# Four more transposed chunks go through the DMA queue: two of the last attention's output, two of the next x

## The chip, the cores and the metric

The kernel runs on one core of a Trainium2 chip. The metric is the device time of one execution in microseconds (us), the median over several runs. The profile is of one execution; its span goes from the first to the last instruction.

Five engines work side by side, each on its own list of instructions in a fixed order: TensorE (PE, with its weight loads PEld), VectorE (DVE), ScalarE (ACT), GpSimd (POOL) and SyncE (SP), which here only issues DMAs. An instruction that must wait for another engine or for a DMA holds up everything behind it on its own engine.

## What is computed

```python
def reference(A_x, A_wqkv, A_wo, B_x, B_w1, B_w2):
    xn = layernorm(A_x)                       # 2048 x 640
    q, k, v = split(xn @ A_wqkv)              # 32 heads of 20
    idx = pos[:, None] - 2 * arange(8)[None]  # window of 8, dilation 2, masked below 0
    attn = softmax(einsum("bhsd,bhswd->bhsw", q, k[idx]) * 20 ** -0.5)
    s = einsum("bhsw,bhswd->bhsd", attn, v[idx]) @ A_wo
    g = silu(silu(xn @ B_w1) @ B_w2)          # 640 -> 1536 -> 640
    return A_x + s * g
```

`B_x` isn't used. Everything is float32. The kernel gets that accuracy from three products of split numbers: each matrix is held as a high part and a low part (the rest after rounding), and hi x hi, lo x hi and hi x lo are summed in PSUM.

## The kernel before

**Groups.** The 2048 positions are worked in four groups g = 0 to 3 of 512 (4 tiles of 128 rows). For each group comes `qkv_phase` (q, k and v in four quarters of 8 heads, q = 0 to 3, and the attention of each quarter on VectorE), then `ffn_phase` (12 up products, 12 down products). The attention of a group takes longer than its qkv products and runs on beside the group's FFN. The product with `wo` for group g - 1 is therefore done inside the FFN of group g, right after its first up product (`wo_phase`); for the last group it comes at the very end (`wo_last`).

**Turning.** A product wants its left side with the 640 channels on the partitions. So the normalised x and the attention's output O, both 128 rows x 640 channels a tile, must be turned, in five chunks c = 0 to 4 of 128 channels by 512 rows. Each chunk ends as a high part (TH, or OH for O) and a low part (TL, OL) in one of two slots that take turns. There are two ways:

- `split_t` (L620 and after): four 128x128 transposes on TensorE into one of two PSUM banks `rot` (L626); ACT copies the high part out (L630); for x, ACT also copies the whole (L632); DVE subtracts (L633 or L636). The up products use the same two `rot` banks.
- `turn_x`: ACT copies the float32 chunk as two planes of 16-bit halves into a buffer (L656); SP issues one DMA transpose for each plane into another buffer (L660); ACT copies the halves back together into the x tile (L665); ACT makes the high part (L670) and DVE the low part (L671). The buffers are pieces of the gate tile G, five of 512 columns, and one extra tile TURN. G is free from the time when `wo_phase` has multiplied it and POOL has added x to it (L1018) until the gate's silu at the end of the FFN (L1183). `X_BY` names which piece serves as source buffer: chunk 1 uses piece 2, chunk 3 piece 0, chunk 4 piece 1; chunks 0 and 2 use TURN. The result of chunk c lands in piece c.

`X_DMA` says which chunks of the next group's x are turned by DMA: in g = 1 all five, in g = 2 chunks 2, 3 and 4. In g = 0 none. The others are turned on TensorE after down products 1, 3, 5, 7 and 9. The chunks of O are turned on TensorE: those of groups 0 to 2 during the next group's qkv products (`O_AT`), those of g = 3 in its own FFN, chunk 0 after down 5, chunk 1 after down 7, chunk 2 after down 8, and chunks 3 and 4 (`o_rest`, L818) before and in the last up product.

**Weights.** A ring of seven slots holds weight units. When a unit's products end, `w_load` starts the load of the unit seven later: from half copies kept in DRAM by POOL's queue (L562), or from the raw weights with a split on ACT and DVE or POOL.

**Attention on DVE.** Per quarter and pair of tiles: q times k (L719), sum over a head (L722), softmax in small steps, weights times v (L761), and a tree of sums into O (L767, L772, L774). For the pairs named in `SHARED`, the last two sums run on POOL, on the quarter's used-up keys: the plane `KV[q][:, 0]`, seen as `partial(q)`.

**The order.** Nothing of the order is written by hand except TensorE's. Each operation is added with its engine, an estimated duration, what it reads and writes, a priority, an earliest time (`at`) and, for DMAs, its bytes. `Weave.order` then simulates the five engines and lists the operations by simulated start; a locked operation keeps DVE and POOL apart. `Weave.plan` repeats this up to 90 times and adds constraints where TensorE would stand idle in the simulation. `clock[0]` is the sum of the TensorE work added so far. A DMA transpose is simulated as 2.0 us of SP and 8 us on top of the usual landing.

Of the kernel before, what the change touches and what calls it, by code (L numbers as in the profile page):

```python
# [10 lines left out]
U16 = mybir.dt.uint16  # L11
AF = mybir.ActivationFunctionType
# [3 lines left out]
P = 128  # L16
# [5 lines left out]
CQ = HQ * DH  # L22
J = 8
T = 4
TOK = T * P
# [27 lines left out]
OUT_IN = 6.0  # L53
CARRY_AT = 8.0
X_SINGLE = (1,2,)
X_DMA = {1: (0, 1, 2, 3, 4), 2: (2, 3, 4)}
X_BY = {1: 2, 3: 0, 4: 1}
SLOW, ISSUE, SUB_LATE = 8, 2.0, 3
PACE0, PACE = -20.0, 12.0
BACK = {1: 0.0, 2: 40.0}  # L60
QAT = 48
OAT = 16
STORE_Q = 1, 3
# [257 lines left out]
def local_attention_silu_ffn(ctx: ExitStack, tc: tile.TileContext, x, wqkv, wo, w1, w2, out):  # L321
    nc = tc.nc
# [18 lines left out]
    NG = len(groups)  # L341
# [15 lines left out]
    TH = [sb.tile([P, DC * TOK + OAT], F32R, name="th0")]  # L357
# [4 lines left out]
    TL = tiles("tl", 2, [P, DC * TOK + 64], F32R)  # L362
    chunks = lambda tiles, at: [v[:, at:at + DC * TOK].rearrange("p (c n) -> p c n", c=DC) for v in tiles]
    OH, OL = chunks(TH, OAT), chunks(TL, OAT)
    TH, TL = chunks(TH, 0), chunks(TL, 0)
# [6 lines left out]
    KV = tiles("kv", NQ, [P, 2, HALO + T, CQ])  # L372
    Q = tiles("q", NQ, [P, T, CQ])
    E = [v[:, :, CQ - W * HQ:].rearrange("p t (w h) -> p t w h", w=W) for v in Q]
    O = sb.tile([P, T, D], F32, name="o")
    PR = sb.tile([P, 2, W, CQ], F32, name="pr")
    L = tiles("l", 2, [P, T, W, HQ])
    XIN = sb.tile([P, T, D], F32, name="xin")
    G = sb.tile([P, T, D], F32, name="gate")
# [3 lines left out]
    TURN = sb.tile([P, TOK], F32, name="turn")  # L383
# [29 lines left out]
    def act(n, fn, reads, writes, prio, table=None, more=0.0, late=0.0, at=0.0, spans=()):  # L413
        return add("ACT", ac(n) + more, fn, reads, writes, prio, table=table, late=late, at=at, spans=spans)

    def free_for(old, new):

        add("DVE", 0.0, lambda: None, [], list(old) + list(new), 0)
# [8 lines left out]
    clock = [0.0]  # L427
# [214 lines left out]
    def both(k):  # L642
        return [k + (0,), k + (1,)]

    def chunk_span(of, c, write=False):
        return [(of, c * P, (T - 1) * D + (c + 1) * P, write)]

    def piece(tile_of, k):
        return tile_of.rearrange("p t d -> p (t d)")[:, k * TOK:(k + 1) * TOK]

    def turn_x(c, i, at, back):

        keys = [("xin", t) for t in range(T)]
        (a, ka), (b, kb) = (piece(G, X_BY[c]), ("buf", X_BY[c])) if c in X_BY else (TURN, ("turn",)), (piece(G, c), ("buf", c))
        into = XIN[:, :, c * P:(c + 1) * P]
        act(2 * TOK, lambda: nc.scalar.activation(  # L656
            a.bitcast(U16).rearrange("p (h t n) -> p h t n", h=2, t=T), into.bitcast(U16).rearrange("p t (n h) -> p h t n", h=2),
            AF.Copy), keys, both(ka), 150, at=at, spans=chunk_span("x", c))
        for h in range(2):
            dma(lambda h=h: nc.sync.dma_start_transpose(  # L660
                b.bitcast(U16).rearrange("p (h t n) -> p h t n", h=2, t=T)[:, h],
                a.bitcast(U16).rearrange("p (h n) -> p h n", h=2)[:, h]),
                [ka + (h,)], [kb + (h,)], P * TOK * 6, clock[0], ISSUE, SLOW)
        kh, kl = t_keys(i, [c], kinds=["th"]), t_keys(i, [c], kinds=["tl"])
        act(2 * TOK, lambda: nc.scalar.activation(  # L665
            into.bitcast(U16).rearrange("p t (n h) -> p h t n", h=2),
            b.bitcast(U16).rearrange("p (h t n) -> p h t n", h=2, t=T), AF.Copy),
            both(kb) + keys, [("xw", c)], 150, more=0.3, at=back, spans=chunk_span("x", c, True))
        hi, lo = (v[i][:, c, :].rearrange("p (t n) -> p t n", t=T) for v in (TH, TL))
        act(TOK, lambda: nc.scalar.activation(hi, into, AF.Copy), [("xw", c)] + keys, kh, 0)  # L670
        dve(TOK, lambda: nc.vector.tensor_tensor(out=lo, in0=into, in1=hi.bitcast(F32), op=OP.subtract),  # L671
            [("xw", c)] + keys + kh, kl, 0, lock=True, late=SUB_LATE, spans=chunk_span("x", c))

    def tile_spans(of, cs, ts):
        return [(of, t * D + c * P, t * D + (c + 1) * P, False) for t in ts for c in cs]
# [32 lines left out]
    def halo_keys(q):  # L708
        return [("halo", q, 1, 0), ("halo", q, 1, 112), ("halo", q, 2, 0), ("halo", q, 2, 112), ("halo", q, 3, 0),
                ("halo", q, 4, 0)] + [("kv", q, t) for t in range(T)]  # L710
# [93 lines left out]
    def o_chunk(g, c, i):  # L804
        qs = range(c * P // CQ, ((c + 1) * P - 1) // CQ + 1)
        split_t(O, [("o", q, t) for q in qs for t in (0, 2)], c, i, (OH, OL))
# [104 lines left out]
    def qkv_phase(g, i, io):  # L911
        for q in range(NQ):
            if g == 0 and q == 0:
                ps = first_quarter(i)
            else:
                ps = [bank() for t in range(T)]
                for c in range(DC):
                    wh, wl, kh, kl = w_next("q", q, c)
                    for t in range(T):
                        o, kp = ps[t]  # L920

                        def unit(c=c, t=t, o=trio_sums(o), wh=wh, wl=wl):
                            hi, lo = TH[i][:, c, tsl(t)], TL[i][:, c, tsl(t)]
                            vh, vl = trio(wh), trio(wl)
                            nc.tensor.matmul(o, hi, vh, start=c == 0, stop=False)  # L925
                            nc.tensor.matmul(o, lo, vh, start=False, stop=False)  # L926
                            nc.tensor.matmul(o, hi, vl, start=False, stop=c == DC - 1)  # L927
                        pe(3 * mm(3 * CQ), unit, t_keys(i, [c], [t]) + [kh, kl], [kp])
                    w_done()
                    if g:  # L930
                        for k in O_AT.get((q, c), ()):
                            o_chunk(g - 1, k, io)
            if groups[g][0] == 0:
                zero = KV[q][0:2, 0:2 - g, 0:HALO, :]
                add("POOL", 2.0 - g, lambda zero=zero: nc.gpsimd.memset(zero, 0.0), [] if g or not q else ["first"],
                    [("halo", q, 1, 0), ("halo", q, 2, 0), ("halo", q, 3, 0), ("halo", q, 4, 0)], clock[0] if g else 1 + 12 * q)
            for t in range(T):
                evac_qkv(g, q, t, *ps[t])
            halo(g, q)
            attend(g, q)  # L940
        attend(g, NQ)

    def t_keys(i, cs, ts=range(T), kinds=("th", "tl")):
        return [(k, i, c, t) for k in kinds for c in cs for t in ts]
# [37 lines left out]
    def gate(ts, cs):  # L982
        return of(G[:, ts.start] if ts.stop - ts.start == 1 else G[:, ts], cs)

    def gkeys(ts, cs):
        return [("g", t, cs.start) for t in range(ts.start, ts.stop)]
# [158 lines left out]
    def ffn_phase(g, i, ix, io):  # L1145
        if g + 1 < NG:
            behind = [("kv", XQ, 0)] if g else []
            step = 1 if g in X_SINGLE else 2
            for t in range(0, T, step):
                load_x(g + 1, t, step, behind=behind)  # L1150
            for t in range(T):
                ln_stats(t)
            ln_rstd(0, T)
            for t in range(T):
                ln_apply(t)
        ps = None
        by_dma = X_DMA.get(g, ())
        bufs = [("buf", c, h) for c in range(DC) for h in range(2)]
        for kind, f in plan(g):
            if kind == "w1":  # L1160
                up(g, i, f, io)
            elif kind == "wo":
                wo_phase(g - 1, io)
                if g == NG - 1:
                    free_for([("xin", t) for t in range(T)], [("xin", t, c) for t in range(T) for c in (0, CA)])
                for c in range(DC) if by_dma else ():
                    ts = slice(c * TOK // D, ((c + 1) * TOK - 1) // D + 1)
                    free_for(gkeys(ts, slice(0, CA)) + gkeys(ts, slice(CA, D)), bufs[2 * c:2 * c + 2])
                for k, c in enumerate(by_dma):
                    turn_x(c, ix, clock[0] + PACE0 + PACE * k, clock[0] + BACK[g])  # L1170
            elif kind == "x":
                if f not in by_dma:
                    split_t(XIN, [("xin", t) for t in range(T)], f, ix, (TH, TL), XIN[:, :, tsl(f)])
            elif kind == "o":
                o_chunk(g, f, io)
            elif kind == "rest":
                o_rest(g, f, io)
            else:
                ps = ps or tm_banks()
                down(f, ps)  # L1180
        for p, kp, ts, cs in tm_views(ps):
            n = (ts.stop - ts.start) * (cs.stop - cs.start)
            act(n, lambda p=p, ts=ts, cs=cs: nc.scalar.activation(gate(ts, cs), p, AF.Silu), [kp], gkeys(ts, cs) + bufs * bool(by_dma), 0, "silu")  # L1183

    add("POOL", 0.7, consts, [], ["consts"], 0)
    act(1, lambda: nc.scalar.activation(SD[:, 1, 0:1], epst, AF.Sqrt), ["consts"], [("rs", 0)], 0, "sqrt")
# [37 lines left out]
```

## Time and profile before

| | us |
|---|---|
| median of 3 runs | 602.38 (601.88 to 603.2) |
| the profiled execution | 600.52 |
| its span | 598.7 |
| DVE busy | 515.6 |
| ACT busy | 236.9 |
| POOL busy | 163.5 |
| transposes of O on TensorE (L626) | 72 |
| transposes of x on TensorE (L626) | 28 |
| DMA transposes (L660) | 16 |

The profile gives times from the start of the span. A row of a view of groups or of the time line names the line of the code, the engine, the operation, what it writes and reads, and in brackets the idle time before it with what ended that. "SPq" and "POOLq" are the queue's own instructions, such as the issue of a DMA. The granted clock of TensorE is 1.00 throughout. The three later FFN phases lie at about 189 to 284 (g = 1), 335 to 431 (g = 2) and 481 to 576 us (g = 3); the last `wo` product follows from 576.

### The profile page before, as it was taken

How to read it: one execution, taken by the hardware profiler on the slowest of the kernel's cores; microseconds unless marked ns; L12 is line 12 of the kernel's file. 1: busy time of each engine (PE TensorE's matmuls, PEld its weight loads, DVE VectorE, ACT ScalarE, POOL GpSimd, SP SyncE). 2: the span in 40 equal slices, each digit the busy share in tenths (PEclk: the TensorE clock that was granted, in tenths of full speed). 3: DMA queues.
4: the chain of work that ended last, by engine and by line, in shares of the span. 5: the costliest groups of instructions: out<-in, count | busy, mean ns of one | idle time of the engine just before them, and what ended most of it. 6: DMA issues, size and time to landing. Idle time of an engine off the chain costs nothing.

```text
span 598.7 us, 9085 instructions
## 1 busy us (share of the span) xinstructions
PE 593.2 (99%) x3463; PEld 558.4 (93%) x3463; DVE 515.6 (86%) x505; ACT 236.9 (40%) x434; POOL 163.5 (27%) x229
## 2 busy tenths in 40 slices
PE   8999999999999999999999999999999999999997
PEld 7999999999999999999999999999999999999997
DVE  6599999999799978999979999999828799999544
ACT  5447364453546224555324604452412342313230
POOL 5800102233110153433211137433122133441100
PEclk9999999999999999999999999999999999999999
DMA  9999999779999999965699999997689997766652
GB/s 295 305 315 335 323 409 387 299 244 299 275 330 313 324 256 334 250 211 164 184 336 293 308 360 269 274 265 223 211 219 284 295 332 247 242 193 215 198 181 88
DMA packets 74823, 162.90 MB, mean 272 GB/s; under 512 B 14509, under 2 KB 38797, under 8 KB 74781
## 3 DMA queue, kind: packets, MB, share of 16 engines
q1 hardware_dynamic: 54941, 82.62, 47.4%
q0 software_dynamic: 19296, 79.31, 44.5%
q8 instruction: 27, 0.44, 0.3%
q10 hardware_dynamic: 544, 0.41, 0.2%
q14 instruction: 15, 0.12, 0.1%
HBM read 107.91 MB, written 34.16 MB: 237 GB/s over the span
## 4 chain that ended last, share of the span: by engine, by line
PE 98%; DMA 1%; DVE 0%; issue 0%
PE acc L969 22%; PE acc L971 15%; PE acc L925 10%; PE acc L926 10%; PE acc L927 10%; PE rot L1104 9%; PE rot L1106 9%; PE rot L1105 9%; PE acc L875 2%; PE rot L626 2%; DMA xin<-in_A_x_dram 1%; PE rot L859 0%; PE rot L1087 0%; DVE st L844 0%; PE rot L818 0%; DVE gate L1055 0%
## 5 line engine op out<-in xcount | busy, mean ns | idle before, releaser
L925 PE MATMUL acc<-w,th 128*128 128x480 f32 x300 | 110.8, 369 | 0.0
L926 PE MATMUL acc<-w,tl 128*128 128x480 f32 x300 | 109.8, 366 | 0.0
L927 PE MATMUL acc<-w,th 128*128 128x480 f32 x300 | 109.8, 366 | 0.0
L969 PE MATMUL acc<-w,sh 128*128 128x384 f32 x384 | 108.6, 328 | 0.0
L719 DVE TENSOR_TENSOR pr<-q,kv 128x2560 f32<-128x2560 f32 x32 | 90.2, 2819 | 18.1 <-ACT th L630 13.0
L971 PE MATMUL acc<-w,sh 128*128 128x256 f32 x384 | 104.7, 273 | 0.0
L1104 PE MATMUL rot<-th,w 128*128 128x512 f32 x240 | 92.1, 384 | 0.0
L761 DVE TENSOR_TENSOR pr<-q,kv 128x2560 f32<-128x2560 f32 x32 | 90.7, 2834 | 1.1
L1105 PE MATMUL rot<-tl,w 128*128 128x512 f32 x240 | 91.0, 379 | 0.0
L1106 PE MATMUL rot<-th,w 128*128 128x512 f32 x240 | 91.0, 379 | 0.0
L722 DVE TENSOR_REDUCE l<-pr 128x128 f32<-128x2560 f32 x32 | 89.6, 2801 | 0.2
L1117 ACT ACTIVATE sh<-rot 128x512 fp32r<-128x512 f32 x48 | 28.8, 599 | 138.5 <-PE rot L1106 138.4
L562 POOL DMA_DIRECT2D w<-half_w x72 | 38.8, 539 | 156.5 <-PE acc L971 56.8
L971 PEld LDWEIGHTS acc<-w,sh 128*128 128x128 f32 x384 | 73.7, 192 | 0.6
L969 PEld LDWEIGHTS acc<-w,sh 128*128 128x128 f32 x384 | 72.6, 189 | 0.6
L562 POOL DMA_DIRECT2D w<-half_q x52 | 27.8, 535 | 122.9 <-PE acc L927 75.4
L927 PEld LDWEIGHTS acc<-w,th 128*128 128x128 f32 x300 | 56.7, 189 | 4.0
L926 PEld LDWEIGHTS acc<-w,tl 128*128 128x128 f32 x300 | 56.7, 189 | 3.8
L925 PEld LDWEIGHTS acc<-w,th 128*128 128x128 f32 x300 | 56.7, 189 | 3.8
L969 PE MATMUL acc<-w,sl 128*128 128x384 f32 x192 | 55.9, 328 | 0.0
L1119 DVE TENSOR_TENSOR sl<-sf,sh 128x512 fp32r<-128x512 f32 x48 | 42.0, 876 | 14.3 <-ACT sf L1118 14.1
L971 PE MATMUL acc<-w,sl 128*128 128x256 f32 x192 | 52.3, 273 | 0.0
(106 smaller groups left out, 1059.9 us busy)
## 6 DMA issues: line engine op xcount, KB each, us to landing
w<-half_w POOLq DMA_DIRECT2D x72, 640.0 KB, 5.5
w<-half_q POOLq DMA_DIRECT2D x52, 480.0 KB, 4.9
half_w<-w SPq DMA_DIRECT2D x24, 640.0 KB, 6.2
half_q<-w SPq DMA_DIRECT2D x20, 480.0 KB, 6.7
kv<-kv SPq DMA_DIRECT2D x15, 560.0 KB, 8.1
w<-half_wo POOLq DMA_DIRECT2D x10, 640.0 KB, 7.0
kv<-kv SPq DMA_DIRECT2D x15, 420.0 KB, 8.3
gate<-in_B_w_dram SPq DMA_DIRECT2D x16, 320.0 KB, 6.9
```

The costliest lines, as they stand in the source:

```text
L562: add("POOL", 1.0, lambda: nc.gpsimd.dma_start(both, src), [("half", u)], [kh, kl], due + 10, nbytes=2 * n * P * 4)
L719: dve(2560, lambda: nc.vector.tensor_tensor(out=PR, in0=win(qq[:, t:t + 2, :], W, 0), in1=win(kv[:, 0, t:t + 2, :], W, CQ), op=OP.mult), h ...
L722: dve(2560, lambda: nc.vector.tensor_reduce(out=l[:, t:t + 2].rearrange("p t w h -> p (t w h)"), in_=PR.rearrange("p t w (h d) -> p (t w h ...
L761: dve(2560, lambda: nc.vector.tensor_tensor(out=PR.rearrange("p t w (h d) -> p t (w h) d", d=DH), in0=e[:, t:t + 2].rearrange("p t w h -> ...
L925: nc.tensor.matmul(o, hi, vh, start=c == 0, stop=False)
L926: nc.tensor.matmul(o, lo, vh, start=False, stop=False)
L927: nc.tensor.matmul(o, hi, vl, start=False, stop=c == DC - 1)
L969: nc.tensor.matmul(a[t][0][:, :CA].rearrange("p (m h) -> p m h", h=2), st, col_a(w), start=first, stop=last)
L971: nc.tensor.matmul(b[t // 2][0][:, h * CB:(h + 1) * CB].rearrange("p (m h) -> p m h", h=2), st, col_b(w), start=first and h == 0, stop=las ...
L1104: nc.tensor.matmul(to, wh[:, cs], hi, start=c == 0, stop=False)
L1105: nc.tensor.matmul(to, wh[:, cs], lo, start=False, stop=False)
L1106: nc.tensor.matmul(to, wl[:, cs], hi, start=False, stop=c == DC - 1)
```

## The change

1. `X_DMA[2]` becomes all five chunks: in g = 2, x chunks 0 and 1 of the last group are no longer turned on TensorE after downs 1 and 3 but by DMA. `BACK[2]`, the earliest time of the copies back after the `wo` product, goes from 40 to 0 us.
2. `O_DMA` is new: in g = 3, chunks 0 and 1 of O are turned by DMA. Their buffers are two halves of the key plane `KV[c][:, 0]` of quarter c, lent out once its last reader is done (`lend`, `spare`). The copy out comes at the earliest 10 and 25 us after the FFN began, the copy back at 40 and 55. The result is written into OH and OL of the slot that `wo_last` reads.
3. `turn_x` is split into `send` (copy out, two DMA transposes) and `join` (copy back, high part, low part), which `turn_o` uses too. The priority of a DMA transpose on SP is now the time of its own copy plus 2, where it was the TensorE clock at the end of `wo_phase`; that holds for g = 1 as well. `O_OUT` and `O_BACK` of groups 1 and 2 are not used, as `O_DMA` names g = 3 alone.

```diff
-X_DMA = {1: (0, 1, 2, 3, 4), 2: (2, 3, 4)}
+X_DMA = {1: (0, 1, 2, 3, 4), 2: (0, 1, 2, 3, 4)}
+O_DMA = {3: (0, 1)}
+O_OUT = (), (35.0, 55.0), (35.0, 55.0), (10.0, 25.0)
+O_BACK = (), (80.0, 82.0), (80.0, 82.0), (40.0, 55.0)
-BACK = {1: 0.0, 2: 40.0}
+BACK = {1: 0.0, 2: 0.0}
...
+    def send(src, c, keys, of, by, to, at):
+        (a, ka), (b, kb) = by, to
         act(2 * TOK, lambda: nc.scalar.activation(
...
-                [ka + (h,)], [kb + (h,)], P * TOK * 6, clock[0], ISSUE, SLOW)
+                [ka + (h,)], [kb + (h,)], P * TOK * 6, at + 2, ISSUE, SLOW)
+    def join(to, into, kinto, reads, c, i, dest, at, spans=((), ())):
...
+    def turn_o(c, i, by, to, at, back):
+        qs = range(c * P // CQ, ((c + 1) * P - 1) // CQ + 1)
+        send(O, c, [("o", q, t) for q in qs for t in (0, 2)], "o", by, to, at)
+        join(to, by[0].rearrange("p (t n) -> p t n", t=T), both(by[1]), [], c, i, (OH, OL), back)
+
+    def turn_os(g, i, begun):
+        by_dma = O_DMA.get(g, ())
+        for c in by_dma:
+            lend(c)
+        for k, c in enumerate(by_dma):
+            turn_o(c, i, spare(c, 0), spare(c, 1), begun + O_OUT[g][k], begun + O_BACK[g][k])
+        for c in by_dma:
+            lend(c, True)
+
+    def spare(q, k):
+        return KV[q][:, 0].rearrange("p t m -> p (t m)")[:, k * TOK:(k + 1) * TOK], ("spare", q, k)
+
+    def lend(q, back=False):
+        old = [(k, q, t) for k in ("kv", "own", "val") for t in range(T)] + [("partial", q)] + halo_keys(q)
+        new = [k for p in range(2) for k in both(("spare", q, p))]
+        free_for(*((new, old) if back else (old, new)))
...
                 wo_phase(g - 1, io)
                 if g == NG - 1:
+                    turn_os(g, io, begun)
...
             elif kind == "o":
-                o_chunk(g, f, io)
+                if f not in O_DMA.get(g, ()):
+                    o_chunk(g, f, io)
```

More of the change, by code (lines that the diff above doesn't have):

```diff
@@ L649, in piece @@
         return tile_of.rearrange("p t d -> p (t d)")[:, k * TOK:(k + 1) * TOK]
[L651 to L655, printed above, removed]
+    def send(src, c, keys, of, by, to, at):
+        (a, ka), (b, kb) = by, to
         act(2 * TOK, lambda: nc.scalar.activation(
-            a.bitcast(U16).rearrange("p (h t n) -> p h t n", h=2, t=T), into.bitcast(U16).rearrange("p t (n h) -> p h t n", h=2),
-            AF.Copy), keys, both(ka), 150, at=at, spans=chunk_span("x", c))
+            a.bitcast(U16).rearrange("p (h t n) -> p h t n", h=2, t=T),
+            src[:, :, c * P:(c + 1) * P].bitcast(U16).rearrange("p t (n h) -> p h t n", h=2),
+            AF.Copy), keys, both(ka), 150, at=at, spans=chunk_span(of, c))
         for h in range(2):
@@ L662, in turn_x @@
                 a.bitcast(U16).rearrange("p (h n) -> p h n", h=2)[:, h]),
-                [ka + (h,)], [kb + (h,)], P * TOK * 6, clock[0], ISSUE, SLOW)
-        kh, kl = t_keys(i, [c], kinds=["th"]), t_keys(i, [c], kinds=["tl"])
+                [ka + (h,)], [kb + (h,)], P * TOK * 6, at + 2, ISSUE, SLOW)
+    def join(to, into, kinto, reads, c, i, dest, at, spans=((), ())):
+        b, kb = to
         act(2 * TOK, lambda: nc.scalar.activation(
@@ L667, in turn_x @@
             b.bitcast(U16).rearrange("p (h t n) -> p h t n", h=2, t=T), AF.Copy),
-            both(kb) + keys, [("xw", c)], 150, more=0.3, at=back, spans=chunk_span("x", c, True))
-        hi, lo = (v[i][:, c, :].rearrange("p (t n) -> p t n", t=T) for v in (TH, TL))
-        act(TOK, lambda: nc.scalar.activation(hi, into, AF.Copy), [("xw", c)] + keys, kh, 0)
+            both(kb) + reads, kinto, 150, more=0.3, at=at, spans=spans[0])
+        kh, kl = t_keys(i, [c], kinds=["th"]), t_keys(i, [c], kinds=["tl"])
+        hi, lo = (v[i][:, c, :].rearrange("p (t n) -> p t n", t=T) for v in dest)
+        act(TOK, lambda: nc.scalar.activation(hi, into, AF.Copy), kinto + reads, kh, 0)
         dve(TOK, lambda: nc.vector.tensor_tensor(out=lo, in0=into, in1=hi.bitcast(F32), op=OP.subtract),
-            [("xw", c)] + keys + kh, kl, 0, lock=True, late=SUB_LATE, spans=chunk_span("x", c))
+            kinto + reads + kh, kl, 0, lock=True, late=SUB_LATE, spans=spans[1])
+    def turn_x(c, i, by, to, at, back):
+        keys = [("xin", t) for t in range(T)]
+        send(XIN, c, keys, "x", by, to, at)
+        join(to, XIN[:, :, c * P:(c + 1) * P], [("xw", c)], keys, c, i, (TH, TL), back,
+             (chunk_span("x", c, True), chunk_span("x", c)))
+    def turn_o(c, i, by, to, at, back):
[16 more added lines that the diff above has]
+        free_for(*((new, old) if back else (old, new)))
     def tile_spans(of, cs, ts):
@@ L931, in qkv_phase @@
                         for k in O_AT.get((q, c), ()):
-                            o_chunk(g - 1, k, io)
+                            if k not in O_DMA.get(g - 1, ()):
+                                o_chunk(g - 1, k, io)
             if groups[g][0] == 0:
@@ L1156, in ffn_phase @@
         ps = None
+        begun = clock[0]
         by_dma = X_DMA.get(g, ())
@@ L1164, in ffn_phase @@
                 if g == NG - 1:
+                    turn_os(g, io, begun)
+                if g == NG - 1:
                     free_for([("xin", t) for t in range(T)], [("xin", t, c) for t in range(T) for c in (0, CA)])
@@ L1169, in ffn_phase @@
                 for k, c in enumerate(by_dma):
-                    turn_x(c, ix, clock[0] + PACE0 + PACE * k, clock[0] + BACK[g])
+                    by = (piece(G, X_BY[c]), ("buf", X_BY[c])) if c in X_BY else (TURN, ("turn",))
+                    turn_x(c, ix, by, (piece(G, c), ("buf", c)), clock[0] + PACE0 + PACE * k, clock[0] + BACK[g])
             elif kind == "x":
@@ L1183, in ffn_phase @@
             act(n, lambda p=p, ts=ts, cs=cs: nc.scalar.activation(gate(ts, cs), p, AF.Silu), [kp], gkeys(ts, cs) + bufs * bool(by_dma), 0, "silu")
+        if g < NG - 1:
+            turn_os(g, i, begun)
     add("POOL", 0.7, consts, [], ["consts"], 0)
```

## The prediction

> **What bounds the kernel now.** I read the page first, then the waits of PE, then the chain in order of time at the places that the change touches, then the three FFN stretches by windows. The group numbers below are those of the code, g = 0 to 3.
>
> ```profile
> PE 593.2 (99%) x3463; PEld 558.4 (93%) x3463; DVE 515.6 (86%) x505; ACT 236.9 (40%) x434; POOL 163.5 (27%) x229
> PE 98%; DMA 1%; DVE 0%; issue 0%
> ```
>
> TensorE is busy 593.2 of 598.7 us, and 98% of the chain that ended last is TensorE. The waits of PE name only these:
>
> ```profile
> PE rot L831 <- POOL ident masks.py:199: 1.4, 1, 1.4
> PE rot L859 <- DVE xin L849: 0.2, 1, 0.2
> ```
>
> Both lie in the first quarter (warm-up and first tiles). After that TensorE never waits. So the time is a plain sum of TensorE work, and work taken off TensorE comes out of the time in full, unless the replacement makes TensorE wait somewhere.
>
> **What is removed.** Four chunks leave TensorE: x chunks 0 and 1 in the FFN of g = 2, and o chunks 0 and 1 in the FFN of g = 3. Each is four 128x128 transposes. The chain in order of time (start, length) has exactly these four:
>
> ```profile
> 367.73 0.44 PE rot L626 x4
> 384.45 0.44 PE rot L626 x4
> 540.28 0.44 PE rot L626 x4
> 553.78 0.44 PE rot L626 x4
> ```
>
> The chain counts from the end of one piece to the end of the next, so 0.44 is what one chunk takes from TensorE, and 4 x 0.44 = **1.76 us** go. No more than that can be won, since TensorE waits for nothing that could get shorter.
>
> **What is added, on ACT and DVE.** The groups by form:
>
> ```profile
> L630 ACT ACTIVATE th<-rot 128x512 fp32r<-128x512 f32 x25 | 14.9, 596 | 57.8 <-PE rot L626 57.8
> L632 ACT ACTIVATE xin<-rot 128x512 f32<-128x512 f32 x7 | 4.1, 592 | 0.0
> L633 DVE TENSOR_TENSOR tl<-xin,th 128x512 fp32r<-128x512 f32 x7 | 4.8, 685 | 1.4 <-ACT xin L632 1.4
> L656 ACT ACTIVATE gate<-xin 128x1024 uint16<-128x1024 uint16 x5 | 5.2, 1050 | 2.7 <-POOL xr L1018 2.7
> L665 ACT ACTIVATE xin<-gate 128x1024 uint16<-128x1024 uint16 x8 | 10.9, 1366 | 0.0
> L670 ACT ACTIVATE th<-xin 128x512 fp32r<-128x512 f32 x8 | 5.1, 632 | 0.3
> L671 DVE TENSOR_TENSOR tl<-xin,th 128x512 fp32r<-128x512 f32 x8 | 6.0, 744 | 0.0
> ```
>
> A chunk turned by DMA costs ACT 1.05 + 1.37 + 0.63 = 3.05 us. An x chunk gives back 0.60 + 0.59, so g = 2 gains 2 x 1.86 = 3.7 us of ACT; an o chunk gives back 0.60, so g = 3 gains 2 x 2.45 = 4.9. DVE gains about 0.06 a chunk. The three FFN stretches (length, then busy time of PE, PEld, DVE, ACT and POOL, granted clock, DMA share, GB/s):
>
> ```profile
> 189.00:284.00 95.00, 95.00 (x592) 90.17 (x591) 85.20 (x70) 41.74 (x59) 34.25 (x48) 1.00 0.95 260
> 335.00:431.00 96.00, 96.00 (x599) 91.15 (x599) 91.01 (x71) 39.55 (x58) 35.05 (x49) 1.00 1.03 276
> 481.00:576.00 95.00, 95.00 (x596) 90.13 (x595) 84.72 (x73) 27.99 (x44) 28.75 (x43) 1.00 0.75 231
> ```
>
> ACT is busy 40 of 96 us in the second and 28 of 95 in the third, so it has room; the PE column is full in all three. The first stretch, g = 1, already turns all five chunks by DMA with the same steps, and PE waits for nothing there. That is the nearest row for g = 2, and I cost the ACT and DVE work at **0**. The cover is the lead of each up product over its down product. Gone it is where ACT sits in a wait with a silu (L1117) queued behind it: a rival below. The changed priorities on SP touch g = 1 too, with the same instructions: 0, and no further bound than the rivals'.
>
> **What is added, on SP and the DMA engines.** Eight transposes, two per chunk:
>
> ```profile
> L660 SPq DMA_TRANSPOSE gate<-turn x6: 1202/1438/1930, 215.2 to 367.6; - x6
> gate<-gate SPq DMA_TRANSPOSE x10, 8.5
> ```
>
> Each holds SP 1.2 to 1.9 us and lands about 8.5 us after issue. In g = 3 SP has nothing to issue between these two rows, and o of heads' quarter 1 is whole when POOL ends its last sum:
>
> ```profile
> 485.14 2.06 SPq L1011 DMA_DIRECT2D xr<-in_A_x_dram  x3
> 523.86 0.87 POOL L774 TENSOR_TENSOR o<-kv 128x320 f32<-128x320 f32 x1
> 563.00 0.33 SPq L1028 DMA_DIRECT2D pr<-in_A_x_dram  x1
> 575.86 0.49 ACT L1183 ACTIVATE gate<-acc 128x384 f32<-128x384 f32 x1 [2.91 <-PE acc L969]
> ```
>
> The later chunk (o 1) then runs 524.7 + 1.05 (copy) + 2.9 (two issues) + 8.5 + 1.37 + 0.63 + 0.74 = about 540. Its reader, the last wo product, comes after the gate's first silu at 575.9: 36 us of margin. The keys of quarters 0 and 1, which lend their planes, have their last reader at the same 524.7. Cost 0.
>
> In g = 2 the readers are the products of g = 3. In g = 1 the last subtraction of a turned chunk, and the first gate silu of that stretch, were
>
> ```profile
> 277.49 0.68 DVE L671 TENSOR_TENSOR tl<-xin,th 128x512 fp32r<-128x512 f32 x1
> 281.65 0.49 ACT L1183 ACTIVATE gate<-acc 128x384 f32<-128x384 f32 x1 [6.20 <-PE acc L969]
> 428.10 0.49 ACT L1183 ACTIVATE gate<-acc 128x384 f32<-128x384 f32 x1 [1.48 <-PE acc L969]
> 430.93 0.53 POOL L562 DMA_DIRECT2D w<-half_q  x1 [2.76 <-PE acc L971]
> 433.37 0.53 POOL L562 DMA_DIRECT2D w<-half_q  x1 [1.91 <-PE acc L927]
> ```
>
> Moved by 428.10 - 281.65 = 146.45, it ends at about 424.6. TensorE enters g = 3 at about 430.9 and takes 2.44 us a chunk (the two POOL rows, each let go by a finished unit), so chunk 4 is read at 440.7: 16 us of margin. Cost 0.
>
> **The one thin margin** is a weight load in g = 2. The ring has seven slots, so a load that starts when a unit ends is for the unit seven later. The load at 368.03 follows the second down product and is for down 5. The rows: the load; the landings of the loads issued between 365.5 and 368.5, and of all loads from 180 to 300 (g = 1); SP beside it; a window; and the end of a down unit, 3.29 before the one at 430.93:
>
> ```profile
> 368.03 0.53 POOL L562 DMA_DIRECT2D w<-half_w  x1 [1.83 <-PE rot L626]
> DMA to landing us min/median/max: 8.8/11.7/14.7
> DMA to landing us min/median/max: 3.5/5.1/8.9
> 366.13 2.96 SPq L660 DMA_TRANSPOSE gate<-turn  x2
> 372.00:376.00 4.00, 4.00 (x20) 3.52 (x19) 3.90 (x4) 1.08 (x2) 2.40 (x4) 1.00 1.32 73
> 427.64 0.53 POOL L562 DMA_DIRECT2D w<-half_q  x1 [2.76 <-PE acc L971]
> ```
>
> The second row holds two loads: the earlier one landed after 8.8, the later one, with two transposes issued beside it, after 14.7, at 382.7. From 372 to 376 the DMA engines moved 73 GB/s, against 276 in the whole stretch, and were busy all along. Down 5 comes after the turn of x 1 (384.45 + 0.44 = 384.89) and one down product (3.29): at 388.2. With both turns gone it comes at 387.3, which leaves 387.3 - 382.7 = **4.6 us**. Now chunk 0's two transposes stand where chunk 2's stood and chunk 1's two follow. What these two more cost the load has no row. Least: 0, since in g = 1, where the same five chunks are turned, no load took over 8.9. Most by the row: 14.7 - 8.8 = 5.9 again, a stall of 1.3. I take no stall, as g = 1 is the nearer row in what it turns; the end of 1.3 goes into the range.
>
> The Trainium skill, "Advanced Engine Details and Errata", section "X-Bar Transpose (TRN2)", holds transposing DMAs to be as fast as regular ones. By that rule the two added would take the load well under 2 us and the margin would stay. The 73 GB/s beside the transposes speak against it.
>
> Two waits are moved. POOL's add of row 3 waits for an x load that SP issues behind the first transposes, and a weight load stands behind the add; on SP the x loads for the last wo product (L1049) wait for the last subtraction:
>
> ```profile
> 369.89 0.35 SPq L1017 DMA_DIRECT2D xr<-in_A_x_dram  x1
> 383.40 1.55 POOL L1018 TENSOR_TENSOR xr<-xr,gate 128x640 f32<-128x640 f32 x1 [1.41 <-DMA xr<-in_A_x_dram]
> 387.51 0.57 POOL L562 DMA_DIRECT2D w<-half_w  x1
> SPq L1049 <- DVE tl L671: 23.7, 2, 17.6
> ```
>
> Two more issues put the x load 2.9 us back and the weight load to 390.4. It is for the unit seven after the one that ended at 384.45, due six units of 3.29 later, at 404.2; with a landing of 8.8 it is there at 399: cost 0 (with one of 14.7, 0.9 us, which the range holds). Behind L1049 stand the carry loads and key shifts of g = 3; those need quarter 0's products, which end five chunks after 430.9, at 443, and the last subtraction moves to 424.6: 0.
>
> **Sum.** 598.7 - 1.76 = 596.9 for the span of the profiled execution, 600.52 - 1.76 = 598.8 with what lies around it. The median of the runs shown is 602.38, 1.86 above that execution, and moves by the same amount: **600.6 us**, 0.29% faster. About 0.2% (1.2 us) is what a measurement of this kernel can tell from no change.
>
> **Rivals.** For the second, a silu in the run of ups 3, 4, 5 of g = 2, and how long ACT stood free before it:
>
> ```profile
> 377.97 0.60 ACT L1117 ACTIVATE sh<-rot 128x512 fp32r<-128x512 f32 x1 [2.15 <-PE rot L1106]
> ```
>
> - *The weight of down 5 lands late.* Place and price as above. With 5.9 more it stalls 1.3: 602.38 - 1.76 + 1.3 = 601.9 (chance 0.13). If four transposes in one wave cost twice that, 11.8, the stall is 7.2 and the time 607.8, **slower** (0.06). It decides from 4.6 us of extra delay, eats the gain at 6.4 and is slower by 0.2% at 7.6. For it: DMA share 1.03 in g = 2 against 0.95 in g = 1. Against it: g = 1 itself.
> - *ACT waits with a silu behind it.* The added copies wait for POOL (L1018 in g = 2, L774 in g = 3) or for a landing. With three ups in a row, the bank of the first must be emptied before the third starts: 2.15 us stand free between two silus there. A return copy and the th copy (1.37 + 0.63 = 2.0) fit; two pairs (4.0) don't: 1.9 lost, 602.5 (0.08).
> - *A turn by DMA is the slower way.* If x turns came onto the path, each would last 1.05 + 8.5 + 1.37 + 0.63 + 0.74 = 12.3 from copy to subtraction, and chunks 3 and 4 wait for 0 and 1 to come back. Two more rounds, 24.6, against 16 of margin: 8.6 lost, 609.2 (0.02). The Trainium skill, "VectorE: DVE Perf Modes", "Rules for kernel authors", speaks for this one: a 128x128 transpose belongs on TensorE where PSUM will do as its place. By the 390 and 1309 ns a block of the section "The three transpose paths", 16 blocks would lose an estimated 14.7 us. The trace has a block at 0.44 / 4 = 0.11 us on TensorE and nothing of the DMA turns on its path.
> - *It does not do what it says:* the list scheduler re-plans all orders, and the waits that come back eat the gain: 602.4 (0.03).
>
> **How the numbers follow.** Forecast 0.68. The runs before spread from 601.88 to 603.2, so half a microsecond either way belongs to each case. Faster by over 0.2%: 0.66 of the forecast and 0.04 of the mild late weight, 0.70. Within: 0.02 + 0.09 + 0.07 + 0.03 = 0.21. Slower: 0.09. The range runs from 600.0 (the forecast less its spread) to 602.6 (the mild late weight and the ACT wait), and leaves out some 0.1.
>
> **What would show it.** Right: no PE wait after the first quarter; 16 fewer L626 transposes; 24 DMA transposes instead of 16; ACT up by some 8.6 us; the last products 1.7 us earlier. Wrong: a PE idle before a down product near 385 to 390 with a weight load as releaser; a silu behind a waiting copy; a first product of g = 3 that waits for a subtraction.

## The result, and the profile after

The change made the kernel **slower**: 609.89 us (median of 5 runs, 604.96 to 613.28) against 602.38, a ratio of 1.0125 (95% interval 1.0098 to 1.0152). Five runs of the kernel before lie between 600.50 and 603.20. The forecast was 600.6, with a range of 600.0 to 602.6. The ratios here and below leave out executions that lie over 1.5% above the same kernel's fastest, so where a kernel's runs spread widely its ratio lies below that of the medians. The profiled execution is the slowest of the five (613.28 us). Its span is 611.5 us, 12.8 more than before, where the medians differ by 7.5, and TensorE does wait now.

The page of the changed kernel, with TensorE's part of the span and the chain that ended last:

```profile
PE 595.3 (97%) x3447; PEld 559.2 (91%) x3447; DVE 513.7 (84%) x505; ACT 245.8 (40%) x440; POOL 163.6 (27%) x229
PE 89%; DMA 4%; issue 3%; SPq 2%; ACT 1%; DVE 0%; POOL 0%; ACTq 0%; POOLq 0%
```

The 16 transposes are gone (3447 matmuls, from 3463), and yet PE is busy 2.1 us longer. PE's idle time, span less busy, grew from 5.5 to 16.2 us. The 10.7 more of idle time and the 2.1 more of busy time make the 12.8. The waits of PE name the idle time:

```profile
PE rot L1140 <- DMA w<-half_w: 7.4, 1, 7.4
PE acc L960 <- ACT gate L1224: 3.2, 1, 3.2
```

One wait of 7.4 us before an up product, for a weight; one of 3.2 before the first product of g = 3, for the gate's silu, which must empty the PSUM banks. The extra busy time goes with the clock. Windows of the changed kernel (the last three columns are granted clock, DMA share and GB/s):

```profile
388.00:392.00 4.00, 2.65 (x20) 2.40 (x18) 4.00 (x4) 3.77 (x4) 0.19 (x1) 1.00 1.14 206
392.00:396.00 4.00, 0.00 (x0) 0.00 (x0) 3.44 (x3) 0.00 (x0) 0.00 (x0) 0.84 1.10 144
396.00:400.00 4.00, 1.99 (x5) 1.63 (x6) 0.00 (x0) 0.82 (x1) 0.00 (x0) 0.50 1.30 298
400.00:404.00 4.00, 4.00 (x17) 3.38 (x16) 0.00 (x0) 1.90 (x4) 2.47 (x3) 0.81 1.50 56
444.00:448.00 4.00, 4.00 (x17) 3.55 (x16) 3.90 (x4) 0.42 (x1) 0.53 (x1) 0.77 0.84 250
```

Behind each wait the granted clock is down, to 0.50 in the worst window, where it was 1.00 throughout before. The removed transposes took 1.76 off TensorE's work and it still grew by 2.1, so the low clock cost about 3.9, found as the difference. The sum: 7.4 + 3.2 + 3.9 - 1.8 = 12.7 of the 12.8. The Trainium skill, "TensorE: Matmul & The Clock Gate", section "Why this matters for your kernels", warns that an idle gap of over some 3 us between matmuls puts TensorE back to half speed; this trace agrees, 0.50 after a gap of 7.4.

Where the weight was late: the loads that POOL issued between 374 and 375, and who waited for them.

```profile
  PE rot L1140: 7.4, 1
DMA to landing us min/median/max: 23.9/24.5/25.1
```

Issued at 374.0, it landed 23.9 us later, at 397.9, and was due at about 390.6. Before, the same load left at 373.4 and took 11.1, and the slowest load of this stretch took 14.7. SP's time line tells what ran beside it (start, length from first to last, with waits between):

```profile
364.82 3.84 SPq L662 DMA_TRANSPOSE gate<-turn  x2
368.75 0.54 SPq L1056 DMA_DIRECT2D out_dram<-xr  x1
369.39 12.40 SPq L662 DMA_TRANSPOSE gate<-gate  x2
...
400.42 7.32 SPq L662 DMA_TRANSPOSE gate<-gate  x2
407.78 3.93 SPq L1056 DMA_DIRECT2D out_dram<-xr  x1
412.10 10.80 SPq L662 DMA_TRANSPOSE gate<-gate  x2
```

Two transposes held SP for 2.96 us before (366.13); here the second pair holds it 12.4, a later pair 10.8. The transposes are slow themselves, and so are the loads beside them. The stretch of g = 2 in one row, to be held against 1.03 and 276 GB/s before:

```profile
335.00:431.00 96.00, 88.64 (x531) 83.10 (x530) 81.51 (x62) 36.42 (x50) 34.24 (x46) 0.96 1.23 245
```

More busy DMA engines, fewer bytes. The second wait is the same slowness in another place. The chain in order of time has the landing of the last chunk's transposes, and ACT's time line what stood behind it:

```profile
414.64 22.01 DMA gate<-gate
```

```profile
436.73 1.37 ACT L670 ACTIVATE xin<-gate 128x1024 uint16<-128x1024 uint16 x1 [6.32 <-DMA gate<-gate]
...
441.81 2.62 ACT L1224 ACTIVATE gate<-acc 128x384 f32<-128x384 f32 x6
```

The transposes landed after 22 us, not 8.5. ACT stood 6.3 us in front of the copy back, with an exp and the gate's silu (L1224) queued behind it, and g = 3 could not start. (The exp and the silu each needed a table load of 1.28 us first, at 438.79 and 440.51.)

In g = 3 the four transposes of O did no harm: each held SP for 1.2 to 1.6 us, and the waits of PE name nothing there.

```profile
L662 SPq DMA_TRANSPOSE kv<-kv x4: 1189/1316/1572, 512.1 to 540.5; - x4
```

### The profile page after: what moved, and what is told of

Read it like the earlier page. It is cut to its first block, busy times and chain, and to the rows that moved or that the text cites. A ratio compares the mean times of both kernels' runs of the same rounds, so it can differ in the third digit from the quotient of the medians.

```text
span 611.5 us, 9075 instructions
## 1 busy us (share of the span) xinstructions
PE 595.3 (97%) x3447; PEld 559.2 (91%) x3447; DVE 513.7 (84%) x505; ACT 245.8 (40%) x440; POOL 163.6 (27%) x229
## 4 chain that ended last, share of the span: by engine, by line
PE 89%; DMA 4%; issue 3%; SPq 2%; ACT 1%; DVE 0%; POOL 0%; ACTq 0%; POOLq 0%
PE acc L1005 20%; PE acc L1007 13%; PE acc L960 10%; PE acc L961 10%; PE acc L962 10%; PE rot L1140 7%; PE rot L1142 7%; PE rot L1141 7%; DMA gate<-gate 4%; PE acc L910 2%; PE rot L629 1%; SPq L662 1%; SPq L1056 1%; DMA xin<-in_A_x_dram 1%; PE rot L894 0%
## 5 line engine op out<-in xcount | busy, mean ns | idle before, releaser
L1155 DVE TENSOR_TENSOR sl<-sf,sh 128x512 fp32r<-128x512 f32 x48 | 39.0, 812 | 23.5 <-ACT sf L1154 23.5
L1140 PEld LDWEIGHTS rot<-th,w 128*128 128x128 f32 x240 | 45.8, 191 | 13.5 <-DMA w<-half_w 7.6
```

The costliest lines, as they stand in the source:

```text
L1140: nc.tensor.matmul(to, wh[:, cs], hi, start=c == 0, stop=False)
```

## The experiments

All runs stand against the kernel before on the same chip, whose median was 601.3 to 601.6 there. The theories, as the expectations number them: **1**, transposing by DMA slows the loads beside it; **2**, the mere bytes of four more DMAs in a full stretch; **3**, the order on SP, with the x load of row 3 behind the transposes and POOL behind that; **4**, the O part in g = 3; **5**, ACT's copies back. Later 1a, 1b and 1c divide theory 1.

### One part at a time

```diff
 # o_only, against the changed kernel
-X_DMA = {1: (0, 1, 2, 3, 4), 2: (0, 1, 2, 3, 4)}
+X_DMA = {1: (0, 1, 2, 3, 4), 2: (2, 3, 4)}
-BACK = {1: 0.0, 2: 0.0}
+BACK = {1: 0.0, 2: 40.0}
 # x_only, against the changed kernel
-O_DMA = {3: (0, 1)}
+O_DMA = {}
```

> Only the two chunks of the last attention go by DMA; x of g = 2 is turned as before (chunks 2, 3, 4 by DMA, BACK 40). Theory 1 (the DMA transposes of g = 2 slow the weight loads beside them): two turns of 0.44 us leave TensorE and no wait comes in, so 602.4 - 0.9 = 601.5, ratio about 0.9985. Theory 4 (the turns of O in g = 3 cost something too, by DMA or by waits on ACT): at or above 602.4.

> Only the x part: all five chunks of g = 2 by DMA, O of g = 3 on TensorE. Theories 1, 2 and 3 (transposes, bytes, order on SP, all in g = 2): the waits of PE before an up product of g = 2 and before the first products of g = 3 come back, time 609.9 + 0.9 = 610.8 or within the spread of the changed kernel, 605 to 614. Theory 4: near 601.5.

`o_only`: 600.61 against 601.54, ratio 0.9991 (0.9979 to 1.0003). The 0.9 us expected is there in the median; the interval just includes no change. No wait of PE came in after the first quarter. `x_only`: 606.17, ratio 1.0048 (1.0011 to 1.0084), ten runs from 600.0 to 612.6. So the loss sits in the x part, and it is not the same in every execution: two of ten had none. The profiled one, at 609.5, had PE wait on a weight again; the second row has the landings of the loads from 340 to 420:

```profile
PE rot L1140 <- DMA w<-half_w: 5.1, 1, 5.1
```

```profile
DMA to landing us min/median/max: 4.4/12.7/23.0
```

Theory 4 is out.

### Transposes, or bytes and order

```diff
 # plain_g2, in send(), for g == 2
-dma(lambda h=h: nc.sync.dma_start_transpose(b...[:, h], a...[:, h]),
+dma(lambda h=h: nc.sync.dma_start(b...[:, h], a...[:, h]),
     [ka + (h,)], [kb + (h,)], P * TOK * 6, at + 2, ISSUE, SLOW)
 # dummy_g2
-if f not in by_dma:
+if f not in by_dma or g == 2 and f < 2:     # and no join for chunks 0 and 1
```

> As x_only, but the ten transposes of g = 2 are plain DMA copies of the same 128 KB each, between the same buffers, from the same queue, in the same order; so x of the last group is not turned and its rows come out as other numbers. Theory 1 (transposing is what slows the loads): no wait of PE, 602.4 - 0.9 = 601.5. Theory 2 (four more DMAs' bytes in a stretch that is full): the weight still lands some 20 us after its issue and the time stays at 608 to 611. Theory 3 (order and issue on SP, with the x load of row 3 behind them): the POOL wait of some 13 us on the x load and the time stay as well, at 607 or more.

> As x_only, but x chunks 0 and 1 of g = 2 are also turned on TensorE as before, and the results of their four DMA transposes are read by nobody: the copies out and the transposes stay, the copies back are gone. Theory 1: the weight loads beside them land 20 us and more after their issue and PE waits, 602.4 + 7 or more = 609 to 613. Theory 5 (it is the ACT copies back, waiting with a silu or the gate behind them): near 602.4, with no late weight.

`plain_g2`: 600.15, ratio 0.9979 (0.9969 to 0.9989), all ten runs between 599.7 and 601.1. Same buffers, bytes, queue and order, and the loss is gone. The loads of its g = 2 (340 to 420), and two windows:

```profile
DMA to landing us min/median/max: 3.4/5.6/11.6
```

```profile
368.00:372.00 4.00, 4.00 (x29) 3.92 (x28) 3.96 (x5) 2.86 (x3) 1.26 (x3) 1.00 1.08 398
372.00:376.00 4.00, 4.00 (x20) 3.49 (x20) 3.90 (x4) 1.09 (x2) 2.87 (x4) 1.00 1.09 384
```

The same windows of the changed kernel:

```profile
368.00:372.00 4.00, 4.00 (x29) 3.87 (x28) 3.97 (x5) 3.03 (x4) 1.07 (x3) 1.00 2.54 207
372.00:376.00 4.00, 4.00 (x20) 3.52 (x19) 3.90 (x4) 1.09 (x2) 3.07 (x4) 1.00 0.74 82
```

207 and 82 GB/s with transposes, 398 and 384 with copies of the same bytes. Theories 2 and 3 are out. A low rate alone is not the loss, though. The kernel before, with two transposes there in place of four, moved 285 and 73 GB/s in these windows (first row here, and the 372 row in the prediction), and `x_dma4`, of the next section, 47 a little later (second row). In neither trace did TensorE wait.

```profile
368.00:372.00 4.00, 4.00 (x30) 3.92 (x29) 3.96 (x4) 2.67 (x4) 1.73 (x3) 1.00 1.25 285
376.00:380.00 4.00, 4.00 (x20) 3.49 (x20) 4.00 (x5) 1.08 (x2) 0.53 (x1) 1.00 1.14 47
```

`dummy_g2`: 608.58 (four runs, 605.8 to 616.3), ratio 1.0105 (1.006 to 1.015). The four added transposes, read by nobody, cost the loss without the gain. Its profiled execution, at 606.3, had PE wait 2.4 for a weight, with a load of 21.6:

```profile
PE acc L1007 <- DMA w<-half_w: 2.4, 1, 2.4
```

```profile
DMA to landing us min/median/max: 5.5/11.0/21.6
```

Theory 5 is out as the main cause: the four copies back are not needed for it.

### Which transposes, beside what

In the changed kernel the transposes of g = 2 go out in two waves: chunks 0 and 1 from 364.8, the others from 396.1. g = 1 turns five chunks too and loses nothing. What differs in g = 2? There SP stores the halves of wo to DRAM (five times 640 KB, issued from 329.9 to 343.5); POOL's load at 355.94 had waited 3.6 us for such a store before the change, and six weight loads went out from there to 368.03, in 12 us, around the first transposes at 366.13 (POOL's time line of the kernel before):

```profile
355.94 0.57 POOL L562 DMA_DIRECT2D w<-half_w  x1 [3.57 <-DMA half_wo<-w]
```

```diff
 # wo_store_g1: units of wo are stored at their first split, in g = 1
-return 1 + (u[0] == "wo" or u[0] == "q" and u[2] in STORE_Q)
+return 1 + (u[0] == "q" and u[2] in STORE_Q)
 # wo_store_g3: at their third, in g = 3
+return 3 if u[0] == "wo" else 1 + (u[0] == "q" and u[2] in STORE_Q)
 # plain_first: as plain_g2, for chunks 0 and 1 alone
 # x_dma4
-2: (0, 1, 2, 3, 4)}
+2: (0, 2, 3, 4)}
 # late1: the copy out of chunk 1 of g = 2
-clock[0] + PACE0 + PACE * k
+clock[0] + (25.0 if g == 2 and c == 1 else PACE0 + PACE * k)
```

All of these have O on TensorE.

> As x_only (five chunks of g = 2 by DMA, O on TensorE), but the split halves of wo are stored to DRAM in g = 1 and loaded in g = 2, where x_only stores them in g = 2: five stores of 640 KB and five raw loads of 320 KB leave the first part of g = 2 and five loads of 640 KB come in; g = 1 gets the five stores. Theory 1b (transposes slow the loads only where these already queue, and the stores of wo with POOL's wait for them make that queue): no wait of PE in g = 2, loads beside the transposes land within 12 us, time 0.9 under before, 600.7; if the queue merely moves, the waits stand in g = 1 in place of g = 2. Theory 1a (ten transposes in one FFN are too many in g = 2 whatever else runs): as x_only, 606, with loads of over 20 us.

> As x_only, but the four transposes of chunks 0 and 1 of g = 2 are plain DMA copies of the same bytes, and the six of chunks 2, 3 and 4 stay; so two chunks of the last group's x are not turned. If the four added transposes are what costs, the six that the kernel before had too leave no wait, and the time is 0.9 under before, 600.7. If the loss needs only the later wave (six in a row, where the kernel before had two and four apart), the weight loads at 390 to 410 stay late and the time is 603 or more.

> As x_only, but chunk 1 of g = 2 goes back to TensorE: eight transposes by DMA in g = 2, one turn of 0.44 us saved. Theory 1: between the two, some runs with a wait, some without: 601 to 606; without any wait it would be 0.4 under before, 601.1.

> As x_only, all five chunks of g = 2 by DMA, but chunk 1 is sent 45 us later, so that only chunk 0's two transposes stand in the first wave (as in x_dma4) and eight stand in the second. Theory 1c (only the transposes beside the burst of late weight loads at 356 to 376 tip the queue): no wait on a weight, 0.4 under x_dma4, 599.7; the chain of chunks 1 and 4 gets longer and may wait at the end of g = 2. Theory 1a (ten transposes are too many wherever they stand): 603 or more, with loads of over 20 us.

> As x_only (five chunks of g = 2 by DMA, O on TensorE), but wo is split again from its raw rows in g = 2 and stored in g = 3: the five stores of 640 KB leave the first part of g = 2 and nothing comes in for them there. Theory 1b (ten transposes are harmless unless weight loads queue beside them): no wait of PE in g = 2, loads beside the transposes within 13 us, time 0.9 under before or better, 600.6 or less. Theory 1a (ten transposes in one FFN are too many by themselves): 606 as x_only, with loads of over 20 us.

`wo_store_g1`: 615.66 (four runs, 613.1 to 616.9), ratio 1.0226 (1.0189 to 1.0262). It is worse, and the place where it loses is the point. Its PE waits at the end of g = 1, behind a copy back of ACT:

```profile
PE acc L960 <- ACT gate L1224: 11.0, 1, 11.0
```

The chain of that execution goes through the landing of the last transposes of g = 1:

```profile
269.62 21.72 DMA gate<-gate
```

And the loads from 180 to 300 (first row) and from 340 to 420 (second) landed in

```profile
DMA to landing us min/median/max: 4.1/10.2/15.9
```

```profile
DMA to landing us min/median/max: 4.1/7.0/12.3
```

With the stores in g = 1, its loads took up to 15.9 us (8.9 before) and its last pair of transposes landed after 21.7, where g = 1 had cost TensorE no wait in any profile so far. The ten of g = 2 stopped delaying weights. The comparison is not clean: the new order also starts the transposes of g = 1 at 231.9, where `x_only` starts them at 215.4, and how much of the 11.0 us belongs to that isn't shown.

`wo_store_g3`: median 600.15 against 601.34; nine runs from 599.6 to 601.5 and one at 608.25, so the ratio with its interval, 1.0 (0.9973 to 1.0027), says nothing either way. Its profiled execution has ten transposes in g = 2, no wait of PE after the first quarter, and loads (340 to 420) of

```profile
DMA to landing us min/median/max: 3.9/6.4/11.9
```

So the count of ten alone doesn't make the loss: theory 1a is out as it was put, and 1b stands. What stalled the one run at 608.25 has no trace. Whether it is the stores themselves that matter or POOL's wait for them, which bunches the six loads, these runs don't separate.

`plain_first`: 599.96, ratio 0.9976 (0.9965 to 0.9987). Six transposes in a row later in g = 2 do no harm, the four in front do. `x_dma4`: 600.09, ratio 0.9977 (0.9967 to 0.9986), all runs within 599.7 and 600.9. Taking chunk 1's two transposes out of the first wave is enough. It was expected between the other two kernels, and that was a miss: the time has an edge. The landings seen show none; the slowest load from 340 to 420 took 14.7 us before, 16.9 in `x_dma4` and 23.0 in `x_only`. The edge comes where a load takes longer than its lead over TensorE.

```profile
DMA to landing us min/median/max: 3.8/9.1/16.9
```

`late1`: 601.34, ratio 0.9996 (0.9973 to 1.0018), runs from 599.8 to 605.1. Its edit does less than was expected of it: the earliest time of the copy moves by 33 us, from -8 to 25 us from the end of `wo_phase`, and chunk 1's transposes went out only 8.6 us later than in `x_only` (first row `x_only`, second `late1`), ahead of the second wave.

```profile
368.08 5.08 SPq L662 DMA_TRANSPOSE gate<-gate  x2
376.65 3.40 SPq L662 DMA_TRANSPOSE gate<-gate  x2
```

That was enough to take most of the loss away, but not all of it, and the expected 599.7 was missed. Its profile is of one of its faster runs, 600.21: the copies back wait up to 5.1 us for their landings, loads take up to 18.5, and TensorE waits for none. What held the slower runs isn't shown, and theory 1c is not decided.

### A gain that is too large

`plain_first` and `x_dma4` won 1.4 and 1.3 us in the medians, where their turns give 0.87 and 0.44.

> As the kernel before (chunks 2, 3, 4 of g = 2 by DMA, O on TensorE), with BACK of g = 2 at 0 instead of 40 and the new priority of the transposes. x_dma4 won 1.3 where its one turn is 0.44. If the earlier copies back are worth the other 0.9, this one is at 600.5; if the two are worth nothing, it is the kernel before, 601.4.

`x3_back0`: 601.62 against 601.6, ratio 0.9989 (0.9973 to 1.0004). By the medians the earlier copies back and the new priority are worth nothing; the interval would still hold the 0.9 us. Its profile shows a wait of PE at the first up product of g = 3, for the last subtraction of O:

```profile
PE rot L1140 <- DVE tl L639: 0.8, 1, 0.8
```

The chain goes back from there through the attention on DVE to the landing of a key shift (L728). Such small waits would explain why the kernel before spreads from 600.3 to some 603 (one run reached 605.6) and its profiled execution, which had none, lies 1.9 under its median. No slower run of that kernel has a trace, so this isn't shown. Whether `x_dma4` wins its extra 0.9 by avoiding them wasn't tried, and stays open.

### Versions that beat both

```diff
 # x4_o2, against the changed kernel
-X_DMA = {1: (0, 1, 2, 3, 4), 2: (0, 1, 2, 3, 4)}
+X_DMA = {1: (0, 1, 2, 3, 4), 2: (0, 2, 3, 4)}
 # wo_g3_full, against the changed kernel
-return 1 + (u[0] == "wo" or u[0] == "q" and u[2] in STORE_Q)
+return 3 if u[0] == "wo" else 1 + (u[0] == "q" and u[2] in STORE_Q)
```

> Chunk 1 of g = 2 stays on TensorE (x chunks 0, 2, 3, 4 by DMA), and O chunks 0 and 1 of g = 3 go by DMA as in the change. Theory 1: both parts are free of waits, so the gains add: x_dma4 measured 0.9977 and o_only 0.9991, together 0.9968, about 599.5 against a kernel before at 601.4; by TensorE's work alone 3 x 0.44 = 1.3, 600.1.

> The whole change with the stores of wo's halves in g = 3. Theory 1b: both parts pay, 0.9 for x and 0.9 for O, 601.5 - 1.8 = 599.7 or a little less; the stores now stand beside the four transposes of O in g = 3, where DMA has room. If the queue moves to g = 3 with them: late wo loads or late O turns there and 602 or more.

`x4_o2`: 599.5 against 601.6, ratio 0.997 (0.9953 to 0.9987); ten of its eleven runs lie between 599.1 and 601.7, and one, of which there is no trace, took 669.98. `wo_g3_full`: 599.69 against 601.34, ratio 0.9971 (0.9959 to 0.9982), six runs from 599.2 to 599.9: by the medians 1.65 of the 1.76 us that the change was to save. Its profiled execution, of span 597.6, has no wait of PE after the first quarter, and its loads of g = 2 landed in

```profile
DMA to landing us min/median/max: 3.7/6.3/13.9
```

## Why the prediction was wrong

- **What bounds the kernel, and the 1.76 us.** Right for the profiled execution. 16 matmuls went, and where nothing waits the time falls by about their time: in the medians `o_only` by 0.9, `wo_g3_full` by 1.65. "No more than that can be won" doesn't hold for the median: `plain_first` won 1.4 where its turns give 0.87.
- **ACT and DVE at 0.** Right for the room. Wrong for the place in one case: the rival "ACT waits with a silu behind it" came true at the end of g = 2, for 3.2 us, with the gate's silu and not an up's. Its price there had been 1.9.
- **The O part at 0.** Right; 36 us of margin were more than enough.
- **The x chunks' margin of 16 us, by g = 1 moved by 146.45.** Wrong in its times. It took the landing of g = 1, 8.5; in g = 2 the last one took 22, and the copy back stood at 436.7, where g = 1's last one moved by 146.45 would stand at 418.5. No product waited for a chunk, though: the last subtraction ended at 442.1, and g = 3 began at 442.35 and reads chunk 4 last. The price came from the silu behind the copy back.
- **The weight margin of 4.6 us, "I take no stall".** This is the step that failed. The row beside it said that two transposes added 5.9 us to a load in this very stretch, and I set it aside for g = 1 as "the nearer row in what it turns". It is nearer in what it turns, and farther in what runs beside: `wo_store_g1` moved the half stores into g = 1, and g = 1 lost. The sum also looked at one load only. Down 5 itself was in time by some 2 us (its load landed after 17.2, at 385.3); the next unit's load, for up 6, took 23.9 in place of 11.1, 12.8 more, and stalled PE for 7.4. The rival with the chance of 0.06 priced a stall of 7.2 and 607.8. That it comes so near 7.4 is luck: it gave 11.8 more to down 5's load, which took 2.5 more, and it left out the clock and the wait of 3.2.
- **The clock.** Not in the sum at all: about 3.9 of the 12.8. A rival that stalls TensorE for several microseconds should have been priced with the low clock behind it.
- **POOL behind the x load of row 3.** The x load was to leave 2.9 us later; it left 12.0 later (381.88 against 369.89), as the slow transposes held SP, and POOL waited 13.3 for it in place of 1.4 (its add began at 401.53). The weights issued behind it were not the ones that PE waited for, and `plain_g2` keeps that order without loss; there the x load left at 370.73.

## What to carry to other kernels

An operation that moves from the bound engine to a DMA takes its price from what the DMA queues hold at that moment, so look for the row of the same transfer beside the same traffic, and believe it over a quieter one elsewhere in the kernel. Where a load's margin is smaller than what one more transfer has been seen to add, the forecast is the stall, and a stall of TensorE had a second cost here, in the clock. A loss of this kind can be bought back by moving other traffic out of the stretch, here the stores of wo, and not only by taking the change back.

## What the runs showed of the hardware

- **A transposing DMA beside queued loads is far dearer than its bytes.** Ten transposes of 128 KB each in g = 2: loads of up to 23 us (`x_only`). Ten plain copies of the same bytes: 11.6. Ten transposes without the stores: 11.9 and 13.9 (`wo_store_g3`, `wo_g3_full`). The Trainium skill's "as fast as regular DMAs" ("Advanced Engine Details and Errata", "X-Bar Transpose (TRN2)") does not hold here beside queued loads. Where nothing was late, a transpose of O in g = 3 held SP for 1.2 to 1.6 us, a plain copy of the same size in `plain_g2` for 0.5 to 0.9.
- **Slow transposes hold their issuing queue.** A pair took SP 2.96 us before and 12.4 in the changed kernel, so the DMAs behind it left late as well.
- **The time has an edge; the landings seen have none.** Two transposes in the first wave: ten runs within 1.1 us, the slowest load 16.9 (`x_dma4`). Four: ten runs over 12.6 us, the slowest load 23.0 (`x_only`). Each landing is that of one execution. How the transposes and the loads get in each other's way inside the DMA engines isn't shown by these traces, and stays open.
